# First chunk handed over from SBUF to SBUF at every step of the first batch's head, and weight sums on VectorE

## The chip, the cores and the metric

One NeuronCore of a Trainium2 chip runs the whole kernel. The metric is the device time of the program in microseconds; a time of "the kernel" is the median of several executions. The profile is of one further execution.

## What is computed

Two blocks stand one behind the other: a filter in the frequency domain over each sequence (8 batches of 3008 tokens, 256 channels), and a gated feed-forward block over all 24064 tokens (width 256 to 1536 and back). All is float32; the three weights arrive as float64.

```python
def _attn_ref(x, filt_r, filt_i):            # x: (8, 3008, 256)
    X = np.fft.rfft(x, axis=1)
    F = (filt_r + 1j * filt_i)[None, :, :]
    y = np.fft.irfft(X * F, n=x.shape[1], axis=1)
    return y.astype(np.float32)

def _moe_ref(x, w_gate, w_val, w_out):       # x: (24064, 256)
    g = x @ w_gate
    silu = g * (1.0 / (1.0 + np.exp(-g)))
    val = x @ w_val
    return (silu * val @ w_out).astype(np.float32)
```

## The kernel before

**The spectral part.** A sequence of 3008 = 47 x 64 tokens is transformed in stages of small matrix products. Stage 1 does the transforms of length 47. Stage 2 does those of length 64 for 24 frequencies `s`, two at a time: twelve middle steps `u` (`N_TWO`). `stage2a` (line 873) multiplies by the table `tb[..., 0]`, and VectorE applies the filter (`f0` holds it); `stage2b` (line 909) multiplies by `tb[..., 1]` and so goes back. Its result, 128 rows of two frequencies, is copied by ScalarE from PSUM to a buffer `g` (four of them, used in turn) and stored to a DRAM tensor `d2`. Stage 3 (`stage3`, line 935) goes back over the length 47, in four chunks of tokens, two halves each; it reads `d2` with another grouping of rows (`load_t4`, line 662), 96 rows of 4 token positions to a half. A chunk yields `y`, the transposed tokens that the feed-forward block works on.

**The head of the first batch.** Nothing of the feed-forward block can start before chunk 0 of batch 0 is through stage 3. The loop at line 1227 runs the twelve steps with `stage2b` four steps behind `stage2a`. For steps 0 to 7 the store to `d2` is issued on the queue of SyncE (SP), for 8 to 11 on ScalarE's. The rows of chunk 0 get into `f0` (which the filter no longer needs there) in three ways: after the loop's last `stage2a` two loads from `d2` are issued for rows 0 to 63 (steps 0 to 7), behind the loop two for rows 64 to 87 (steps 8 to 10), and the last step writes its eight rows straight from `g` to `f0`, in eight transfers of 8 KB, in turn on ScalarE's and SP's queue (line 923). So a row of steps 0 to 10 goes to DRAM and comes back. In a row of `g` lie chunks, halves and token positions in the order of the table.

**What else stands in the head.** `idle` (line 585) issues matrix products that compute nothing. Four of them on a tile of zeros stand behind the loop, and two more on the weight sums `A13` and `A01`, which therefore wait for these sums.

**Preparation of the weights.** The float64 weights are loaded in halves (`load_weights`, line 377) and rounded to float32 in a chain of small operations on VectorE, ScalarE and GpSimd (`round_half`, line 388). For the hidden weights, sums of blocks are kept as well: `combine_weights` (line 460) makes for each of six pairs a sum A, on VectorE, partly with a product on ScalarE, and then B and E. B is computed on GpSimd; E on VectorE for four pairs of the first weight group and on GpSimd otherwise. `Preparation` (line 487) writes this out in ticks: each operation has a tick, each weight follows the last by 4 ticks, and the first of the `w_out` weights by 12. `finish(step)` runs all ticks that are due by a step; `tick` runs one. Ahead of stage 3, `finish(0)` and four more ticks are run. In the main loop (line 1380) the order of all engines is written out in `SCHEDULE`; 20 ticks are spread over it for each step, in step 0 only behind the place `A01`.

**The main loop.** A step is one chunk with one of three groups of hidden columns. `P`, `Q`, `A`, `B`, `E` are products of `y` or of sums of `y` (`combine_sequence`, line 989) with weights; `W` are the products with `w_out`. Each engine takes its instructions in program order, and so do the queues of SP and ScalarE on which transfers are issued.

Of the kernel before, what the change touches and what calls it, by code (L numbers as in the profile page):

```python
# [41 lines left out]
FP32 = mybir.dt.float32  # L42
# [6 lines left out]
B, S, C = 8, 3008, 256  # L49
# [5 lines left out]
NS, NQ = 24, 64  # L55
# [69 lines left out]
def dft_tables():  # L125
# [26 lines left out]
    d[0, :, :, 1] = (-sn * sg).transpose(0, 2, 1)  # L152
    d[1, :, :, 1] = (c * sg).transpose(0, 2, 1)
    d = d.reshape(128, NS, 128)
    de = np.stack([d, d.transpose(2, 1, 0)], 2)

    hi = 2 * np.pi * (np.outer(2 * n1 + 1, s) % (2 * N1)) / (2 * N1)
    scale = np.where(s == 0, 1.0, 2.0) / S
# [45 lines left out]
def kernel(  # L204
# [120 lines left out]
    def add(eng, dst, a, b):  # L325
        return eng.tensor_tensor(out=dst, in0=a, in1=b, op=ALU.add)  # L326

    def sub(eng, dst, a, b):
        return eng.tensor_tensor(out=dst, in0=a, in1=b, op=ALU.subtract)  # L329
# [130 lines left out]
    def combine_weights(g, i, j):  # L460

        d = j - i
        wt_f = weights_of(0, 0, g).rearrange("p s z f -> p s (z f)")
        m = wt_f[:, SLOT[f"A{i}{j}"]]
        ui, uj, yi, yj = [wt_f[:, SLOT[f"{p}{q}"]] for p in "PQ" for q in (i, j)]
        if d == 1:
            pin(negated_sum(m, ui, uj))
        else:
            pin(add(nc.vector, m, ui, uj))
        yield  # L470
        if d > 1:
            pin(nc.scalar.mul(m, m, -1.0 / d))
        yield
        pin(sub(nc.gpsimd, wt_f[:, SLOT[f"B{i}{j}"]], yi, m))
        early = g == 0 and PAIRS_USED.index((i, j)) < 4
        pin(add(nc.vector if early else nc.gpsimd, wt_f[:, SLOT[f"E{i}{j}"]], yj, m))

    def keep_weights(g, piece):

# [7 lines left out]
    class Preparation:  # L487
# [3 lines left out]
        def __init__(self):  # L491
# [9 lines left out]
            for i, (_, (use, *at)) in enumerate(weights):  # L501
                hid, g = use == "hid", at[0] if use == "hid" else at[0] // JB
                by = ((0, 3, 6) if hid else (1, 4, 7))[g]
                b = base[-1] + (4 if i != 2 * len(BLOCKS) else 12) if i else 0
                if i >= N_EARLY:
                    same = [n for n in range(N_EARLY, i) if spot_of(n) == spot_of(i)]
                    k = 2 if spot_of(i) is None else 1
                    last = base[same[-k]] + 8 if same[k - 1:] else 0
                    b = max(b, last + 8)
                    put(max(last, b - 10), lambda i=i: load_weights(i), by)  # L510
                base.append(b)
                if hid and g == NG - 1:
# [78 lines left out]
    class Spectral:  # L591


        def __init__(self, b):
# [3 lines left out]

            self.d2_tokens = self.d2.rearrange("a n c -> (a n) c").rearrange(
                "(n a) c -> n a c", n=N2)  # L600
            self.d2_rows = self.d2.rearrange("a (h n) c -> (a h) n c", h=2)
            self.x, self.t2, self.f, self.tb, self.p, self.t4, self.y = {}, {}, {}, {}, {}, {}, {}
            self.real = {}

# [54 lines left out]
            for u in range(i * n // NV, (i + 1) * n // NV):  # L659
                self.tb[u], self.f[u] = tb0[:, ts(u, NV)], f0[:, ts(u, NV)]  # L660

        def load_t4(self, k, i, part=None):
            if part is not None:

                t = f0[0:NK, ts(i, NH), :]
                r = (slice(0, 64), slice(64, NK - 4 * NV))[part]
                self.load(out=t[r], in_=self.d2_rows[r, ts(i, NH), :])
            else:
                t = t4pool.tile([128, NH, C], FP32, name=f"t4_{self.b}_{k}_{i}", tag="t4")
                at = 2 * k + i  # L670
                if self.b == 0:
                    self.load(out=t[0:NK], in_=self.d2_rows[:, ts(at, NH), :])
                else:

                    rows = self.d2_tokens.rearrange("(h n) a c -> h (n a) c", h=2)
                    rows = rows[:, ts(at, 2 * NS * NH)]
                    for j in range(2):
                        self.load(out=t[64 * j:64 * j + 64, 1],
                                  in_=rows[j, 128 * (1 - j):128 * (1 - j) + 64])
                        self.load(out=t[:, 2 * j], in_=rows[j, 64 * j:64 * j + 128])  # L680
            self.t4[k, i] = t

        def bank(self, name):
# [225 lines left out]
        def stage2b(self, u):  # L909
# [5 lines left out]
                                     rhs=pt[:, i, :], start=True, stop=True))  # L915
            g = self.place("g", u)
            yield
            if self.b == 0 and u == N_TWO - 1:
                for i in range(NV):
                    pin(nc.scalar.copy(out=g[:, i], in_=ps[:, i]))  # L920
                for j in range(4 * NV):
                    i, at = j // 4, 64 * (j // 2 % 2) + 32 * (j % 2)
                    pin((nc.scalar, nc.sync)[j % 2].dma_start(
                        out=f0[4 * NV * u + j:4 * NV * u + j + 1, 0:2 * NH],
                        in_=g[at:at + 2 * NH, i:i + 1]))
            else:
                pin(nc.scalar.copy(out=g, in_=ps))
            queue = nc.scalar if self.b or u >= 8 else nc.sync
            if self.b == 0:
                pin(queue.dma_start(out=self.twos(self.d2, u), in_=g))  # L930
                return
            rows = self.d2_tokens.rearrange("n (p s) c -> (n p) (s c)", p=2)
            pin(queue.dma_start(out=rows[:, ts(u, NV * C)], in_=g.rearrange("q s c -> q (s c)")))

        def stage3(self, k, step):

# [240 lines left out]
    with tc.tile_pool(name="start", bufs=1) as spool0:  # L1177
# [49 lines left out]
        for u in range(N_TWO + lag):  # L1227
# [116 lines left out]
    for b in range(B):  # L1344
# [35 lines left out]
        for step in range(NCHUNK * NG + (b == B - 1)):  # L1380
# [98 lines left out]
```

## Time and profile before

| | |
|---|---|
| median of three runs | 2825.01 us (2822.03 to 2826.37) |
| the profiled execution | 2828.65 us, span of its instructions 2826.7 us |
| PE busy (TensorE matmul) | 2786.0 us, 99% |
| DVE (VectorE) | 1993.1 us, 71% |
| ACT (ScalarE), POOL (GpSimd) | 1564.5 us, 55%; 1578.1 us, 56% |
| head of batch 0: last product of the middle steps starts | 60.05 us |
| first product of stage 3 (`wpd`) | 70.21 us |
| first product of the feed-forward block (`wk`) | 76.82 us |

Times inside the profile count from its first instruction. In a timeline a line has the start, the duration, the engine, the line of the code, the operation, the tile written and the tiles read, and the count of instructions merged; the idle time before it and what ended it stand in brackets. SPq and ACTq are the queues on which SP and ScalarE issue transfers; such a line's duration is the time of issue, not that of the transfer. Names of tiles are the program's, so that `f<-d` is a load of `d2` into `f0`, `d<-x` a store of `g` (which lies in the tile `x0`) to `d2`, `f<-x` the transfer from `g` to `f0`, and `t<-d` a load for a later chunk.

### The profile page before, as it was taken

How to read it: one execution, taken by the hardware profiler on the slowest of the kernel's cores; microseconds unless marked ns; L12 is line 12 of the kernel's file. 1: busy time of each engine (PE TensorE's matmuls, PEld its weight loads, DVE VectorE, ACT ScalarE, POOL GpSimd, SP SyncE). 2: the span in 40 equal slices, each digit the busy share in tenths (PEclk: the TensorE clock that was granted, in tenths of full speed). 3: DMA queues.
4: the chain of work that ended last, by engine and by line, in shares of the span. 5: the costliest groups of instructions: out<-in, count | busy, mean ns of one | idle time of the engine just before them, and what ended most of it. 6: DMA issues, size and time to landing. Idle time of an engine off the chain costs nothing.

```text
span 2826.7 us, 48513 instructions
## 1 busy us (share of the span) xinstructions
PE 2786.0 (99%) x15444; PEld 2318.8 (82%) x15444; DVE 1993.1 (71%) x4567; ACT 1564.5 (55%) x4182; POOL 1578.1 (56%) x1683
## 2 busy tenths in 40 slices
PE   8999999999999999999999999999999999999998
PEld 6877878788888888888888888888888888888887
DVE  7898766767667766677766677667676767666666
ACT  5775445555555555555555555555555555555554
POOL 4886575465545654456644566444665455545544
PEclk9999999999999999999999999999999999999999
DMA  9687866877666776667666676667766777654543
GB/s 238 210 275 248 274 215 213 281 221 235 192 184 203 246 221 180 198 212 237 218 185 197 214 242 205 186 192 233 230 207 178 217 222 226 194 149 151 152 137 82
DMA packets 363477, 586.59 MB, mean 208 GB/s; under 512 B 198444, under 2 KB 246380, under 8 KB 363128
## 3 DMA queue, kind: packets, MB, share of 16 engines
q1 hardware_dynamic: 337962, 534.70, 60.9%
q10 hardware_dynamic: 23470, 45.46, 5.9%
q0 software_dynamic: 1792, 3.34, 0.4%
q8 instruction: 125, 2.05, 0.3%
q14 instruction: 128, 1.05, 0.1%
HBM read 467.81 MB, written 101.34 MB: 201 GB/s over the span
## 4 chain that ended last, share of the span: by engine, by line
PE 88%; POOL 3%; DVE 1%; issue 1%; DMA 1%; ACT 0%; ACTq 0%; SPq 0%; POOLq 0%; DVEq 0%
PE wa L1050 24%; PE wk L1050 16%; PE wA L1147 16%; PE we L1050 12%; PE wG L1147 8%; PE wF L1147 4%; PE pd L953 3%; PE wqa L700 2%; PE wqc L759 1%; PE wqb L771 1%; POOL out_dram L1132 1%; POOL h L329 1%; POOL y_t L326 0%; DMA lent<-later_tbl 0%; POOL h L326 0%
## 5 line engine op out<-in xcount | busy, mean ns | idle before, releaser
L1050 PE MATMUL wa<-y_t,wt_t 128*128 128x188 f32 x4464 | 879.5, 323 | 6.1 <-DMA y_t<-yt 1.9
L1050 PEld LDWEIGHTS wa<-y_t,wt_t 128*128 128x128 f32 x4464 | 747.2, 190 | 83.1 <-ACT wa L1076 10.8
L1050 PEld LDWEIGHTS wk<-y,wt_t 128*128 128x128 f32 x2976 | 496.6, 191 | 110.8 <-issue 33.4
L1050 PE MATMUL wk<-y,wt_t 128*128 128x188 f32 x2976 | 573.5, 326 | 5.0 <-DVE y L326 2.8
L326 POOL TENSOR_TENSOR h<-h 128x376 f32<-128x376 f32 x190 | 183.3, 986 | 694.5 <-DVE h L1097 694.5
L329 POOL TENSOR_TENSOR h<-h 128x376 f32<-128x376 f32 x572 | 558.8, 998 | 15.4 <-DVE h L326 15.2
L1147 PE MATMUL wA<-h,wo_t 128*128 128x376 f32 x1532 | 552.3, 483 | 3.6 <-DVE o L326 3.5
L1050 PE MATMUL we<-y_t,wt_t 128*128 128x188 f32 x2232 | 431.8, 323 | 0.7 <-ACT we L1081 0.7
L329 POOL TENSOR_TENSOR D<-f,f 128x376 f32<-128x376 f32 x288 | 279.8, 986 | 258.6 <-ACT f L1065 258.5
L329 DVE TENSOR_TENSOR we<-we,m 128x376 f32<-128x376 f32 x576 | 319.4, 555 | 136.5 <-PE we L1050 70.1
L1050 PEld LDWEIGHTS we<-y_t,wt_t 128*128 128x128 f32 x2232 | 369.5, 190 | 1.5 <-ACT we L1081 1.2
L1147 PEld LDWEIGHTS wA<-h,wo_t 128*128 128x128 f32 x1532 | 275.5, 190 | 113.3 <-issue 6.2
L1085 ACT COPY m<-wa 128x376 f32<-128x376 f32 x576 | 272.6, 473 | 103.0 <-PE wa L1050 100.2
L333 DVE SCALAR_TENSOR_TENSOR y<-wk,c 128x376 f32<-128x376 f32 x480 | 244.4, 539 | 61.4 <-ACT c L1069 39.0
L1092 ACT ACTIVATE g<-wa 128x188 f32<-128x188 f32 x576 | 187.6, 326 | 165.8 <-PE wa L1050 155.3
L1092 ACT ACTIVATE u<-we 128x188 f32<-128x188 f32 x576 | 188.2, 327 | 160.1 <-DVE we L329 153.3
L1147 PE MATMUL wG<-h,wo_t 128*128 128x376 f32 x768 | 274.0, 479 | 0.0
L1069 ACT COPY c<-wk 128x376 f32<-128x376 f32 x288 | 136.4, 473 | 224.8 <-PE wk L1050 189.2
L1065 ACT ACTIVATE f<-wk 128x376 f32<-128x376 f32 x288 | 140.4, 488 | 171.1 <-PE wk L1050 124.3
L1081 ACT COPY we<-y 128x376 f32<-128x376 f32 x480 | 222.2, 480 | 19.6 <-DVE h L1097 13.9
L1097 DVE TENSOR_TENSOR h<-wa,g 128x188 f32<-128x188 f32 x576 | 198.5, 345 | 37.1 <-ACT g L1092 36.8
L1097 DVE TENSOR_TENSOR h<-we,u 128x188 f32<-128x188 f32 x576 | 197.5, 344 | 26.6 <-ACT u L1092 15.6
(165 smaller groups left out, 3515.5 us busy)
## 6 DMA issues: line engine op xcount, KB each, us to landing
wt_t<-w_all SPq DMA_DIRECT2D x174, 896.0 KB
wt_t<-w_all SPq DMA_DIRECT2D x174, 768.0 KB
lent<-filter SPq DMA_DIRECT2D x36, 1024.0 KB
lent<-d SPq DMA_DIRECT2D x84, 256.0 KB
d<-lent ACTq DMA_DIRECT2D x84, 256.0 KB
d<-lent ACTq DMA_DIRECT2D x96, 192.0 KB
lent<-raw SPq DMA_DIRECT2D x144, 128.0 KB
t<-d SPq DMA_DIRECT2D x112, 128.0 KB
```

Of the source, the lines that this page charges most:

```text
L326: return eng.tensor_tensor(out=dst, in0=a, in1=b, op=ALU.add)
L329: return eng.tensor_tensor(out=dst, in0=a, in1=b, op=ALU.subtract)
L333: return nc.vector.scalar_tensor_tensor(out=dst, in0=a, scalar=-1.0, in1=b, op0=ALU.mult, op1=ALU.subtract)
L953: pin(nc.tensor.matmul(out=rows, lhsT=self.t4[k, i][:, j, ts(cb, 128)], rhs=cols, start=j == 0, stop=True, skip_group_check=True))
L1050: pin(nc.tensor.matmul(out=ps[:, z], lhsT=self.wt[:, SLOT[p], z], rhs=rhs, start=start and z == 0, stop=True, skip_group_check=True))
L1065: pin(act.mul(self.small(f"f{i}", f"f{i}", 1), t[f"k{i}"], -1.0))
L1069: pin(act.copy(out=self.small(f"c{i}", f"c{i}", 1), in_=t[f"k{i}"]))
L1081: pin(act.copy(out=self.bank(f"e{at}"), in_=t[f"y{at}"]))
L1085: pin(act.copy(out=self.small(f"m{at}", "m", 4), in_=t[f"a{at}"]))
L1092: pin(act.activation(out=self.small(op, "g", 3, 1)[:, 0], in_=ps[:, 1], func=AF.Silu))
L1097: pin(v.tensor_tensor(out=dst, in0=ps[:, 0], in1=g, op=ALU.mult))
L1147: pin(nc.tensor.matmul(out=self.tiles[at], lhsT=wo_t[:, JB * q + i, WO[p], :], rhs=self.hs[i][:, HID[p]], start=start and i == 0, stop=Tru ...
```

## The change

The columns of the going-back table are put into another order, so that the 32 rows of one chunk lie together in `g`. Every middle step of batch 0 now writes its rows of chunk 0 from `g` to `f0` itself, in two transfers of 32 partitions to 4 rows (32 KB each). They are issued on SP, only the second one of the last step on ScalarE. The stores to `d2` remain, all on SP, for the other chunks: for steps 0 to 8 right behind the two transfers, for 9 to 11 together behind the loop. The loads of chunk 0 from `d2` and the eight transfers of the last step are gone. In `d2` a row of a chunk has eight token positions side by side, and `load_t4` reads it so.

B and E of the first weight group are computed on VectorE for all six pairs. The four early `w_out` halves are loaded at step 10 of the loop instead of step 6. Four ticks are no longer run ahead of stage 3: the `w_out` weights begin 16 instead of 12 ticks behind the hidden ones, and in step 0 ticks begin behind the place `P0` instead of `A01`. The two idle products on `A13` and `A01` are gone.

```diff
     d = d.reshape(128, NS, 128)
-    de = np.stack([d, d.transpose(2, 1, 0)], 2)
+    chunks = np.arange(128).reshape(2, 2, NCHUNK, NW).transpose(2, 0, 1, 3).ravel()
+    de = np.stack([d, d.transpose(2, 1, 0)[:, :, chunks]], 2)
...
-        pin(sub(nc.gpsimd, wt_f[:, SLOT[f"B{i}{j}"]], yi, m))
-        early = g == 0 and PAIRS_USED.index((i, j)) < 4
-        pin(add(nc.vector if early else nc.gpsimd, wt_f[:, SLOT[f"E{i}{j}"]], yj, m))
+        e = nc.gpsimd if g else nc.vector
+        pin(sub(e, wt_f[:, SLOT[f"B{i}{j}"]], yi, m))
+        pin(add(e, wt_f[:, SLOT[f"E{i}{j}"]], yj, m))
...
-                b = base[-1] + (4 if i != 2 * len(BLOCKS) else 12) if i else 0
+                b = base[-1] + (4 if i != 2 * len(BLOCKS) else 16) if i else 0
...
-            self.d2_rows = self.d2.rearrange("a (h n) c -> (a h) n c", h=2)
+            flat = self.d2.rearrange("a n c -> (a n) c")
+            self.d2_parts = flat.rearrange("(s q) c -> q s c", q=128)
+            self.d2_rows = flat.rearrange("(s k a n) c -> k s a n c", k=NCHUNK, a=4, n=NW)
+            self.rest = []
...
-        def load_t4(self, k, i, part=None):
-            if part is not None:
-
-                t = f0[0:NK, ts(i, NH), :]
-                r = (slice(0, 64), slice(64, NK - 4 * NV))[part]
-                self.load(out=t[r], in_=self.d2_rows[r, ts(i, NH), :])
+        def load_t4(self, k, i):
+            t = t4pool.tile([128, NH, C], FP32, name=f"t4_{self.b}_{k}_{i}", tag="t4")
+            at = 2 * k + i
+            if self.b == 0:
+                self.load(out=t[0:NK].rearrange("p (o n) c -> p o (n c)", o=1),
+                          in_=self.d2_rows[k, :, :, ts(i, NH)].rearrange("s a n c -> s a (n c)"))
...
-            if self.b == 0 and u == N_TWO - 1:
+            if self.b == 0:
+                last = u == N_TWO - 1
+                for i in range(0, NV, 1 if last else NV):
+                    n = slice(i, i + (1 if last else NV))
+                    pin(nc.scalar.copy(out=g[:, n], in_=ps[:, n]))
                 for i in range(NV):
-                    pin(nc.scalar.copy(out=g[:, i], in_=ps[:, i]))
-                for j in range(4 * NV):
-                    i, at = j // 4, 64 * (j // 2 % 2) + 32 * (j % 2)
-                    pin((nc.scalar, nc.sync)[j % 2].dma_start(
-                        out=f0[4 * NV * u + j:4 * NV * u + j + 1, 0:2 * NH],
-                        in_=g[at:at + 2 * NH, i:i + 1]))
-            else:
-                pin(nc.scalar.copy(out=g, in_=ps))
-            queue = nc.scalar if self.b or u >= 8 else nc.sync
-            if self.b == 0:
-                pin(queue.dma_start(out=self.twos(self.d2, u), in_=g))
+                    r = 4 * (NV * u + i)
+                    queue = nc.scalar if last and i else nc.sync
+                    pin(queue.dma_start(out=f0[r:r + 4, 0:2 * NH], in_=g[0:4 * NW, i:i + 1]))
+                self.rest.append((u, g))
+                if u < 9:
+                    self.store_rest()
                 return
...
+        def store_rest(self):
+
+            for u, g in self.rest:
+                self.load(out=self.d2_parts[:, ts(u, NV)], in_=g)
+            self.rest = []
...
             if u == 6:
                 pin(nc.sync.dma_start(out=wi_t, in_=wi_dram.ap()))
+            if u == 10:
                 for i in range(8, N_EARLY):
                     load_weights(i)
-            if u == N_TWO - 1:
-                for i in range(2):
-                    spec.load_t4(0, i, 0)
         for i in range(2):
-            spec.load_t4(0, i, 1)
+            spec.t4[0, i] = f0[0:NK, ts(i, NH), :]
+        spec.store_rest()
         for i in range(2):
             spec.load_t4(1, i)
         preparation.finish(0)
-        preparation.tick(0, 4)
 
         idle(zero, [bank("idle") for _ in range(4)], 512)
-        for p in ("A13", "A01"):
-            at = SLOT[p]
-            idle(wt_t[:, at:at + 2].rearrange("p s z f -> p (s z f)"), [bank("idle")], 512)
...
-                        (step or place > SCHEDULE.index("A01")):
+                        (step or place > SCHEDULE.index("P0")):
                     preparation.tick(step)
```

More of the change, by code (lines that the diff above doesn't have):

```diff
@@ L660, in load_tables @@
                 self.tb[u], self.f[u] = tb0[:, ts(u, NV)], f0[:, ts(u, NV)]
-        def load_t4(self, k, i, part=None):
-            if part is not None:
-                t = f0[0:NK, ts(i, NH), :]
-                r = (slice(0, 64), slice(64, NK - 4 * NV))[part]
-                self.load(out=t[r], in_=self.d2_rows[r, ts(i, NH), :])
-            else:
-                t = t4pool.tile([128, NH, C], FP32, name=f"t4_{self.b}_{k}_{i}", tag="t4")
-                at = 2 * k + i
-                if self.b == 0:
-                    self.load(out=t[0:NK], in_=self.d2_rows[:, ts(at, NH), :])
-                else:
[L675 to L680, printed above, removed]
+        def load_t4(self, k, i):
[4 more added lines that the diff above has]
+                          in_=self.d2_rows[k, :, :, ts(i, NH)].rearrange("s a n c -> s a (n c)"))
+            else:
+                rows = self.d2_tokens.rearrange("(h n) a c -> h (n a) c", h=2)
+                rows = rows[:, ts(at, 2 * NS * NH)]
+                for j in range(2):
+                    self.load(out=t[64 * j:64 * j + 64, 1],
+                              in_=rows[j, 128 * (1 - j):128 * (1 - j) + 64])
+                    self.load(out=t[:, 2 * j], in_=rows[j, 64 * j:64 * j + 128])
             self.t4[k, i] = t
@@ L917, in stage2b @@
             yield
-            if self.b == 0 and u == N_TWO - 1:
-                for i in range(NV):
-                    pin(nc.scalar.copy(out=g[:, i], in_=ps[:, i]))
-                for j in range(4 * NV):
-                    i, at = j // 4, 64 * (j // 2 % 2) + 32 * (j % 2)
-                    pin((nc.scalar, nc.sync)[j % 2].dma_start(
-                        out=f0[4 * NV * u + j:4 * NV * u + j + 1, 0:2 * NH],
-                        in_=g[at:at + 2 * NH, i:i + 1]))
-            else:
-                pin(nc.scalar.copy(out=g, in_=ps))
-            queue = nc.scalar if self.b or u >= 8 else nc.sync
-            if self.b == 0:
-                pin(queue.dma_start(out=self.twos(self.d2, u), in_=g))
+            if self.b == 0:
[3 more added lines that the diff above has]
+                    pin(nc.scalar.copy(out=g[:, n], in_=ps[:, n]))
+                for i in range(NV):
+                    r = 4 * (NV * u + i)
[4 more added lines that the diff above has]
+                    self.store_rest()
                 return
+            pin(nc.scalar.copy(out=g, in_=ps))
+            queue = nc.scalar
             rows = self.d2_tokens.rearrange("n (p s) c -> (n p) (s c)", p=2)
             pin(queue.dma_start(out=rows[:, ts(u, NV * C)], in_=g.rearrange("q s c -> q (s c)")))
+        def store_rest(self):
+            for u, g in self.rest:
+                self.load(out=self.d2_parts[:, ts(u, NV)], in_=g)
+            self.rest = []
         def stage3(self, k, step):
```

## The prediction

> **What bounds the kernel now.** First the busy table of the page: TensorE (PE) is busy 2786.0 of 2826.7 us, so only a stretch in which it waits can give anything back. Next the busy times by stretch, for the head of the first batch. Columns: the stretch, its length, then busy us (and instructions) of PE, its weight loads, VectorE (DVE), ScalarE (ACT), GpSimd (POOL), PE's granted clock, DMA share, GB/s.
>
> ```profile
> 62.00:64.60 2.60, 2.60 (x7) 0.83 (x5) 0.00 (x0) 0.30 (x2) 0.00 (x0) 1.00 0.81 217
> 64.60:67.40 2.80, 0.01 (x1) 0.00 (x0) 0.01 (x1) 0.46 (x2) 0.00 (x0) 1.00 0.36 100
> 67.40:70.20 2.80, 2.17 (x4) 0.62 (x5) 2.80 (x4) 1.89 (x5) 2.77 (x4) 1.00 0.75 198
> 70.20:74.00 3.80, 3.78 (x32) 3.63 (x32) 3.80 (x6) 0.83 (x2) 3.80 (x5) 1.00 0.98 254
> 74.00:76.80 2.80, 0.00 (x0) 0.00 (x0) 1.72 (x6) 2.17 (x6) 0.33 (x1) 0.85 0.61 142
> 76.80:80.00 3.20, 3.18 (x13) 3.18 (x14) 1.80 (x4) 1.62 (x4) 1.78 (x2) 0.50 0.00 0
> ```
>
> From 61.0 to 76.8 PE does real work only in 70.2 to 74.0 (the stage-3 products `wpd`); the other 5.8 us that it shows are idle products on zeros and weights. Then the timeline of PE and of ACT says who holds it.
>
> ```profile
> 61.02 3.60 PE L588 MATMUL widle<-room 128*128 128x512 f32 x8
> 67.41 2.17 PE L588 MATMUL widle<-wt_t 128*128 128x512 f32 x4 [2.79 <-ACT wt_t L472]
> 70.21 3.78 PE L956 MATMUL wpd<-wi_t,f 96*128 96x94 f32 x32 [0.63 <-PE widle L588]
> 76.82 1.62 PE L1050 MATMUL wk<-y,wt_t 128*128 128x188 f32 x4 [2.83 <-DVE y L326]
> ```
>
> ```profile
> 61.65 0.65 ACT L920 COPY x<-wpc 128x256 f32<-128x256 f32 x2 [0.51 <-PE wpc L914]
> 62.05 4.17 ACTq L923 DMA_DIRECT2D f<-x  x4
> 66.51 0.38 ACTq L930 DMA_DIRECT2D d<-x  x1
> 66.94 0.42 ACT L472 ACTIVATE wt_t<-wt_t 128x256 f32<-128x256 f32 x1 [4.64 <-DMA f<-x]
> ...
> 74.52 0.51 ACT L419 ACTIVATE pw<-pw,off_t 128x256 f32<-128x256 uint32 x1 [1.12 <-DVE pw L406]
> 75.06 0.51 ACT L421 ACTIVATE pw<-pw,top_t 128x256 f32<-128x256 f32 x1
> 75.60 0.42 ACT L423 ACTIVATE pw<-pw 128x256 uint32<-128x256 f32 x1
> 75.92 0.83 ACT L968 COPY y<-wpd 128x376 f32<-128x376 f32 x2
> ```
>
> Two holds are seen. **The data**: the last `f<-d` loads are issued at 67.40 and 67.87 (SP's timeline), the second for 0.34 us, and `wpd` starts at 70.21, 2.0 us after that issue ended. **The queue of ACT**: its four hand-over transfers and the store keep it 4.64 us from the weight sum L472, on which DVE (5.98 us idle), POOL (8.55) and the second group of idle products wait; and after `wpd` it runs three weight-rounding operations (74.52 to 76.02) before the copy L968 that opens the way to `wk`. The price of a transfer's issue comes from the list of one tile's instructions (ns min/median/max):
>
> ```profile
> L606 SPq DMA_DIRECT2D f<-in_filt_i_dram x6: 311/317/382, 36.8 to 46.1; - x6
> L923 SPq DMA_DIRECT2D f<-x x4: 634/652/772, 62.2 to 66.7; - x4
> ```
>
> And that of a sum on DVE with and without POOL at work beside it (POOL starts at 67.43):
>
> ```profile
> 67.39 0.42 DVE L326 TENSOR_TENSOR wt_t<-wt_t 128x256 f32<-128x256 f32 x1 [5.98 <-ACT wt_t L472]
> 67.73 0.95 DVE L333 SCALAR_TENSOR_TENSOR wt_t<-wt_t 128x256 f32<-128x256 f32 x1
> ```
>
> **What the Trainium skill says.** (1) "TensorE: Matmul & The Clock Gate", "What's actually happening": the clock is halved after an idle window of about 3.4 us, the windows run freely, and a busy one restores it. The trace agrees: the clock is 0.80 over 70 to 80 and 0.86 over 80 to 90, which is 6.8 us at half, two windows. (2) "SBUF — State Buffer", "Who interferes with whom": a DVE instruction with two SBUF inputs contends with GpSimd reads. The trace agrees: 0.42 against 0.95 us. (3) "DMA: Bandwidth & Descriptors", "Why a DMA increments its semaphore by 16 and not by 1": the number of DMA engines is the largest up to 16 that divides the outer dimension of both sides. For a transfer of 32 partitions into 4 that would be 4 engines. No view of before names an engine, so this is open; it carries a rival.
>
> **The change part by part.**
>
> *Hand-overs.* Each of 12 steps now issues two transfers of 32 KB (32 partitions into 4 rows of `f0`), 23 on SP and 1 on ACT; the eight of 8 KB in the last step and the four `f<-d` loads go. What is queued ahead of the last one on SP, from 46.8 us, where SP is done with the table loads: 22 hand-overs, 9 stores (0.37 us and 0.09 to the next, 4.1 us), `wi` and four weight loads (2.2 us). A hand-over's issue isn't shown. Below: 0.32 us, as the 32-row table load; above: 0.65, as the 8-row one. I take 0.36, near the 32-row load and the store, because both have as many rows or more. With 0.09 between: 22 x 0.45 = 9.9, so SP is through at 46.8 + 6.3 + 9.9 = 63.0. (At 0.32: 62.1. At 0.65: 69.4.) The last copy has a second condition: its buffer is that of step 7, whose store sits behind the four weight loads moved from step 6 to step 10. In the window 59 to 62 us, 544 packets of 1 KB took 51.0% of 16 engines' 3 us, 45 ns each, so 256 KB takes 0.72 us: the weights, issued from about 57.4, hold the engines some 2.9 us, and the store of step 7 lands near 63. Copy of one half 0.4, issue 0.36, landing 2.0: **`wpd` starts at 66.0 instead of 70.2**. Within the steps nothing else is bound by it: DVE paces them (0.72 us each for three operations, no idle from 46 to 60).
>
> *Ticks and sums.* The four ticks behind the head go to step 0, after P0 instead of A01 (15 ticks where there were 11). With them the three ACT operations of 74.5 to 76.0 leave the way, and only one rounding operation of DVE stays. B and E sums run on DVE: from the first ACT sum (about 64.5) twelve operations of 0.34 (0.42 less the overlap), 4.1 us, until 68.7; POOL is silent, so none takes 0.95. `wpd` needs 3.6 us and the DVE addition with it 0.4: `wk` at 66.0 + 4.0 = 70.0, where it was 76.8: **-6.8 us**. The cover of the sums is `wpd` itself; were it gone, they would cost up to 1 us. The four sums of the last two pairs cost DVE some 1.4 to 3.8 us in step 0, beside PE's weight-bound first products.
>
> *Clock.* PE's gap shrinks to 64.6 to 66.0, too short for an idle window, although the two idle products on weights are gone. The 28 products of 76.8 to 82.8 ran at 0.31 instead of 0.16 us (0.21 instead of 0.11), 2.9 us. But POOL's four sums (78.2 to 83.2) and its D behind them hold A01 anyway: I take **-1.0** (0 to -2.9).
>
> *Given back.* The first weight of `w_out` starts 4 ticks later, and what is due at step 1 is done there in one piece: seven ticks instead of three. PE waits there already ("PE wF L1147 <- POOL wo_t L438: 1.7, 1, 1.7"), behind POOL's product (0.8 us) and DVE's L426 and L430. I take **+1.0** (0 to +2.5).
>
> *Stores and loads.* The stores of steps 9 to 11 and the loads of chunk 1 follow on SP; loaded at about 70 to 71 instead of 73 to 75, they are covered.
>
> Sum: -6.8 - 1.0 + 1.0 = -6.8. The profiled execution took 2828.65 us (span 2826.7), 3.6 above the median of 2825.0 of three runs; 2821.9 in its terms, **2818** in those of the median.
>
> **Next late** are DVE and POOL: from 86 to 176 they are busy about 84 and 82 of 90 us, PE about 85.
>
> **The rivals.**
> *R1, few engines.* If four engines carry every hand-over, each has 8 packets of 45 ns, 0.36 us: 24 of them 8.6, nine stores 6.5, weights 2.6, sum 17.7 us behind the table loads that fill the engines until about 50.3. The last lands at 69.5. PE is then idle from 64.6 with no product to keep the clock, and `wpd` runs at half for most of its length (5.7 us): `wk` at 75.6, -1.2; clock later -1.0, burst +1.0: 2824. For it: the skill's rule, and a DMA share of 0.9 to 1.0 up to 56 us. Against: the table traffic ends at 51 and the share in 58 to 62 is 0.61.
> *R2, the issue decides: slower.* If a hand-over costs SP 0.65 to 0.8 us, like the 8-row ones, SP is through at 69.4 to 72.8. `wpd` starts at 72.1 to 75.6, at half clock: `wk` at 78.2 to 81.7, +1.4 to +4.9; the burst +1.0; chunk 1, whose loads wait for three stores issued later still, +0 to +1: about 2830. It is slower than before from 0.59 us per issue on. For it: the only SBUF-to-SBUF row of the head. Against: the 32-row rows.
> *R3, lost later.* `wk` comes early, but the full DVE and POOL of 96 to 176 give half of it back: 2821.5.
>
> **Chances.** Forecast 0.55 (2814 to 2820.5), R3 0.07, R1 0.24, R2 0.14. About 0.2% (5.6 us, 2819.4) is what a measurement of this kernel can tell from no change. Of the forecast 0.48 lies beyond it and 0.07 within; R3, R1 and 0.03 of R2 within; 0.11 of R2 beyond. Faster 0.48, same 0.41, slower 0.11. The range runs from 2814 to 2828: it takes in forecast, R3 and R1 and leaves out most of R2.
>
> **What would show it.** Right: issues of `f<-x` on SP near 0.36 us, `wpd` near 66, no half clock before 90, DVE sums of 0.42 ending before `wk` near 70, PE's wait for `wo_t` at step 1 under 3 us. Wrong: SP's issues without a pause up to 69 (R2); packets still moving between issue and a late landing (R1); a PE gap over 3.4 us before `wpd`; new PE waits for DVE or POOL between 90 and 180 (R3).

## The result, and the profile after

The changed kernel takes **2838.83 us** (median of five, 2835.47 to 2839.97) where the kernel before, on the same chip, took 2826.37 (five, 2822.03 to 2828.53): 12.5 us more, ratio 1.0041 with a 95% interval of 1.003 to 1.0053. Forecast was 2818; the range ended at 2828. Its profiled execution took 2839.97 us, with a span of 2838.0.

First PE's timeline of the changed kernel, from the end of the middle steps on (start, duration, line, tiles, count, idle time before it and what ended it):

```profile
61.06 4.25 PE L589 MATMUL widle<-room 128*128 128x512 f32 x8
75.26 7.11 PE L962 MATMUL wpd<-wi_t,f 96*128 96x94 f32 x32 [9.96 <-DMA f<-x]
82.16 1.52 PE L1056 MATMUL wk<-y,wt_t 128*128 128x188 f32 x4
```

`wpd` starts at 75.26 us (70.21 before) and takes 7.11 instead of 3.78; `wk` starts at 82.16 (76.82 before). PE waits 9.96 us for `f<-x`, the hand-overs. Next SP's timeline, and behind it the instructions of the hand-over's line (ns min/median/max):

```profile
59.49 1.32 SPq L925 DMA_DIRECT2D f<-x  x2
60.86 0.44 SPq L610 DMA_DIRECT2D d<-x  x1
61.42 1.34 SPq L925 DMA_DIRECT2D f<-x  x2
62.80 0.44 SPq L610 DMA_DIRECT2D d<-x  x1
63.35 1.84 SPq L387 DMA_DIRECT2D wo_t<-in_moe_w_out_dram  x4
65.28 1.32 SPq L925 DMA_DIRECT2D f<-x  x2
66.65 0.46 SPq L610 DMA_DIRECT2D d<-x  x1
67.22 1.30 SPq L925 DMA_DIRECT2D f<-x  x2
68.57 0.45 SPq L610 DMA_DIRECT2D d<-x  x1
69.12 3.43 SPq L925 DMA_DIRECT2D f<-x  x5
```

```profile
L925 SPq DMA_DIRECT2D f<-x x23: 625/631/830, 47.4 to 71.9; - x23
L925 ACTq DMA_DIRECT2D f<-x x1: 1425/1425/1425, 71.2 to 71.2; - x1
```

A pair of hand-overs takes 1.30 to 1.34 us, a store 0.45, and from 59.5 to 72.55 us no gap is over 0.12 us: SP does nothing but issue. The Trainium skill, "Perfetto Trace Analysis", "DMA Instruction — HWDGE (DVE, Sync)", says that such a line runs from when all semaphores are satisfied to when the sequencer is free again, descriptors generated, and that the movement of data is not in it. The trace agrees: the last hand-over on SP is issued from 71.93 to 72.55 us and its semaphore rises for the last time at 74.92. So 0.63 us is the price on SP itself, not that of the transfer.

The busy times by stretch, here by tens (columns as in the prediction), carry the clock. Before:

```profile
70.00:80.00 10.00, 6.96 (x45) 6.83 (x46) 7.52 (x14) 4.62 (x11) 6.11 (x8) 0.80 0.56 139
80.00:90.00 10.00, 9.98 (x58) 9.62 (x58) 5.97 (x13) 6.55 (x19) 8.02 (x10) 0.86 0.70 248
100.00:110.00 10.00, 8.32 (x43) 6.49 (x42) 10.00 (x21) 7.59 (x21) 9.84 (x12) 1.00 0.66 225
```

Changed kernel:

```profile
60.00:70.00 10.00, 5.11 (x13) 2.03 (x12) 0.98 (x3) 1.76 (x3) 0.00 (x0) 0.94 0.70 230
70.00:80.00 10.00, 4.74 (x22) 4.77 (x23) 3.98 (x12) 2.32 (x6) 0.00 (x0) 0.50 0.37 118
80.00:90.00 10.00, 10.00 (x41) 9.63 (x40) 3.94 (x9) 3.16 (x8) 5.89 (x5) 0.53 0.74 213
110.00:120.00 10.00, 5.17 (x17) 4.07 (x16) 7.70 (x13) 4.90 (x13) 9.42 (x13) 0.66 0.66 237
```

Between 70 and 90 us the clock is 0.50 and 0.53, where it was 0.80 and 0.86. By the trace's clock records it was half from 68.8 to 89.3 us, 20.5 us instead of 6.8, and once more from 113.2 to 120.0 us, where it was full before.

This is not all. Set against the kernel before by the n-th product, PE is about 6.5 us late up to the first product with `w_out` at step 1, 11.9 us late a few us behind it and 11.3 us at the end. PE's timeline there, first the kernel before and then the changed one:

```profile
103.21 0.80 PE L1147 MATMUL wF<-h,wo_t 128*128 128x376 f32 x2
105.69 0.90 PE L1147 MATMUL wF<-h,wo_t 128*128 128x376 f32 x2 [1.68 <-POOL wo_t L438]
```

```profile
109.72 0.80 PE L1153 MATMUL wF<-h,wo_t 128*128 128x376 f32 x2
115.35 1.62 PE L1153 MATMUL wF<-h,wo_t 128*128 128x376 f32 x2 [4.83 <-DMA y<-y]
```

The waits of the changed kernel (us in total, times, longest):

```profile
PEld wF L1153 <- POOL wo_t L439: 5.4, 1, 5.4
PE wF L1153 <- DMA y<-y: 4.8, 1, 4.8
```

In the kernel before they were 2.3 and 1.7. The second line names a DMA; the first, of the same product, names what came last: POOL's product for the rounded weight. POOL's timeline, before:

```profile
99.70 0.77 POOL L438 TENSOR_TENSOR wo_t<-w,pw 128x256 f32<-128x256 f32 x1
100.43 1.37 POOL L326 TENSOR_TENSOR y_t<-y 128x564 f32<-128x564 f32 x1
101.88 1.45 POOL L329 TENSOR_TENSOR y_t<-y_t,y 128x564 f32<-128x564 f32 x1
103.29 1.55 POOL L326 TENSOR_TENSOR y_t<-y_t,y 128x564 f32<-128x564 f32 x1
104.81 0.82 POOL L438 TENSOR_TENSOR wo_t<-wo_t,pw 128x256 f32<-128x256 f32 x1
```

And in the changed kernel:

```profile
108.93 1.38 POOL L327 TENSOR_TENSOR y_t<-y 128x564 f32<-128x564 f32 x1
110.39 1.39 POOL L330 TENSOR_TENSOR y_t<-y_t,y 128x564 f32<-128x564 f32 x1
111.74 1.42 POOL L327 TENSOR_TENSOR y_t<-y_t,y 128x564 f32<-128x564 f32 x1
113.12 0.91 POOL L439 TENSOR_TENSOR wo_t<-w,pw 128x256 f32<-128x256 f32 x1
114.45 0.84 POOL L439 TENSOR_TENSOR wo_t<-wo_t,pw 128x256 f32<-128x256 f32 x1 [0.42 <-DVE wo_t L431]
```

A weight of `w_out` takes two such products, one for each half. Before, the first of the second weight stood ahead of the three sums (99.70 us) and only the second behind them (104.81); now both stand behind, and the second waits for DVE besides. PE went on at 105.69 us before and goes on at 115.35 now, 2.5 and 5.6 us behind the first product with `w_out`. The longer wait is the larger part of this loss. The rest is the clock, at half behind it: from there to the second `wk` (109.86 and 121.78 us) PE takes 6.4 us instead of 4.2.

So there are two losses, one in the head and one at step 1, and each has a wait and a stretch at half clock.

### The profile page after: what moved, and what is told of

Its sections match the earlier page's. It is cut to its first block, busy times and chain, and to the rows that moved or that the text cites. A ratio compares the mean times of both kernels' runs of the same rounds, so it can differ in the third digit from the quotient of the medians.

```text
span 2838.0 us, 48517 instructions
## 1 busy us (share of the span) xinstructions
PE 2790.8 (98%) x15440; PEld 2324.0 (82%) x15440; DVE 1993.3 (70%) x4575; ACT 1565.7 (55%) x4182; POOL 1571.5 (55%) x1675
## 3 DMA queue, kind: packets, MB, share of 16 engines
q14 instruction: 128, 1.05, 0.1%
## 4 chain that ended last, share of the span: by engine, by line
PE 90%; POOL 4%; DMA 3%; DVE 2%; issue 1%; ACT 1%; SPq 0%; ACTq 0%; POOLq 0%; DVEq 0%
PE wa L1056 24%; PE wk L1056 17%; PE wA L1153 16%; PE we L1056 12%; PE wG L1153 8%; PE wF L1153 4%; PE pd L959 3%; PE wqa L699 1%; PE wqc L758 1%; PE wqb L770 1%; POOL out_dram L1138 1%; POOL h L330 1%; DMA f<-in_filt_r_dram 1%; POOL y_t L327 1%; POOL h L327 0%
## 5 line engine op out<-in xcount | busy, mean ns | idle before, releaser
L330 POOL TENSOR_TENSOR h<-h 128x376 f32<-128x376 f32 x572 | 557.6, 997 | 15.4 <-DVE h L327 15.2
L334 DVE SCALAR_TENSOR_TENSOR y<-wk,c 128x376 f32<-128x376 f32 x480 | 244.4, 539 | 58.1 <-ACT c L1075 36.1
```

What stands on the lines that cost most here:

```text
L334: return nc.vector.scalar_tensor_tensor(out=dst, in0=a, scalar=-1.0, in1=b, op0=ALU.mult, op1=ALU.subtract)
```

## The experiments

Each time is a median, with the ratio to the kernel before on the same chip (2826.0 to 2826.7 us) and its 95% interval. The theory: SP's issues delay the head by some 6 us (rival R2 of the prediction), and the moved ticks cost another 5 to 6 at step 1. Rivals: the bytes of the hand-overs on few DMA engines (R1), the landing of the stores, the sums on VectorE, the clock.

### The ticks

**ticks_back** (the changed kernel, three edits undone):

```diff
-  b = base[-1] + (4 if i != 2 * len(BLOCKS) else 16) if i else 0
+  b = base[-1] + (4 if i != 2 * len(BLOCKS) else 12) if i else 0
+        preparation.tick(0, 4)
-  (step or place > SCHEDULE.index("P0")):
+  (step or place > SCHEDULE.index("A01")):
```

> The changed kernel with its weight ticks put back: w_out begins 12 ticks behind, four ticks run ahead of stage 3, and ticks in step 0 begin behind A01. Hand-overs and sums stay. Theory (two separate losses: SP's hand-over issues of 0.63 us in the head, and the postponed ticks at step 1): PE's wait for wo_t at the start of step 1 goes from 4.8 us back to about 2, the first wpd stays near 75.3, the time falls by 3 to 5 us, to about 2834. Rival (the wait at step 1 is only the late head's echo): the wait stays over 4 us and the time within 1 us of the changed kernel's.

2832.79 us, 1.0017 (1.0009 to 1.0025): 6.0 less than the change. PE's wait at step 1 is 1.7 us again, and the head is as late as in the change (`wk` 82.57).

**ticks_12** undoes only the first line of that diff.

> The changed kernel, but w_out begins 12 ticks behind the hidden weights again; the other two edits of the ticks stay (from P0, none ahead of stage 3). If the late begin of w_out is what makes PE wait at step 1, this alone gives back 4 to 6 us (2833 to 2835). If it is that fewer ticks are run ahead of stage 3, so that they pile up in step 0 all the same, under 1 us comes back.

2834.41 us, 1.0029 (1.0018 to 1.0041), 4.4 less, though this interval overlaps that of the change. In its trace PE's wait at step 1 is 1.8 us again and the clock is full there; so, of the three edits, the late begin of `w_out` is the one that makes the wait.

**before_ticks_late** puts the reverse of the three edits into the kernel before.

> The kernel before with only the four ticks moved (w_out begins 16 ticks behind the hidden weights, ticks of step 0 from P0 on, no four ticks ahead of stage 3). If the ticks cost by themselves, PE's wait for wo_t at step 1 grows from 1.7 to about 5 us and the kernel takes 4 to 6 us more (2830 to 2832); the three ACT operations leave the way to wk, which may come up to 1 us sooner. If they cost only together with the late head, the time is within 1.5 us of before.

2832.38 us, 1.0021 (1.0013 to 1.0029): **6.3 us more, from the ticks alone**, in a kernel whose head is nearly as it was (`wk` 77.09; `wpd` runs at half clock here, 7.11 us, but the gap of 2.83 us behind it is gone). Expected were 4 to 6. Its waits:

```profile
PEld wF L1147 <- POOL wo_t L438: 5.5, 1, 5.5
PE wF L1147 <- DMA y<-y: 4.9, 1, 4.9
```

The clock is at half from 108.4 to 115.2 us here too.

### The sums and the clock

**sums_back** (B and E of the first group on the engines of before):

```diff
-  e = nc.gpsimd if g else nc.vector
-  pin(sub(e, wt_f[:, SLOT[f"B{i}{j}"]], yi, m))
-  pin(add(e, wt_f[:, SLOT[f"E{i}{j}"]], yj, m))
+  pin(sub(nc.gpsimd, wt_f[:, SLOT[f"B{i}{j}"]], yi, m))
+  early = g == 0 and PAIRS_USED.index((i, j)) < 4
+  pin(add(nc.vector if early else nc.gpsimd, wt_f[:, SLOT[f"E{i}{j}"]], yj, m))
```

> The changed kernel with B and part of E of the weight sums back on GpSimd as before; nothing else. Theory: the sums lie in a stretch where VectorE waits 12 us for nothing else, so they cost nothing on either engine: within 1 us of the changed kernel. Rival (the four sums that VectorE now does in step 0 feed the late work at step 1): the time falls by 1 to 3 us.

2836.82 us, 1.0039 (1.0026 to 1.0051); its interval and that of the change overlap, and the 2.0 us less would fit the rival's 1 to 3 as well. By the trace little of it is in the head (`wk` 0.2 us sooner), and behind step 1 PE is 12.3 us late against 11.9. Two kernels below (hybrid11_ticks, one_hand_ticks_early) have the sums on VectorE and take no longer than before. So the sums are not where the 12 us went; whether they cost a us or two isn't decided.

**warm** (16 idle products ahead of `wpd` instead of four):

```diff
-  idle(zero, [bank("idle") for _ in range(4)], 512)
+  idle(zero, [bank("idle") for _ in range(16)], 512)
```

> The changed kernel with 16 instead of 4 idle products on zeros ahead of stage 3, so that PE has something to do until about 75; nothing else. Theory (half clock is a consequence worth several us): the clock stays full until wpd, its 32 products take 3.6 instead of 7.1 us, wk starts 3 to 4 us earlier and the time falls by 3 to 5 us. Rival (the short products of wpd do not hold the clock up, whatever runs ahead): wpd is fast, but the clock falls again behind it, and the gain is under 3 us.

2836.32 us, 1.0035 (1.0022 to 1.0047). PE's timeline shows where the gain went:

```profile
75.75 3.78 PE L962 MATMUL wpd<-wi_t,f 96*128 96x94 f32 x32
79.36 0.83 PE L1056 MATMUL wk<-y,wt_t 128*128 128x188 f32 x4
85.64 2.02 PE L962 MATMUL pd<-wi_t,t 96*128 96x94 f32 x8 [5.45 <-DMA t<-d]
```

`wpd` takes 3.78 us and `wk` comes 2.8 us sooner, but PE then waits 5.45 us for chunk 1's rows, whose loads stand behind the last stores, and the clock falls again (84.3 to 91.1 us): PE, 2.5 us late at `wk`, is 8.45 us late some ten us on, where the change is 6.5 late. So the head gained nothing, and the interval overlaps that of the change. Behind the hand-overs, chunk 1's loads are next late.

### What holds the hand-overs

**two_queues** (the second hand-over of every step on ACT's queue):

```diff
-  queue = nc.scalar if last and i else nc.sync
+  queue = nc.scalar if i else nc.sync
```

> The changed kernel with the second hand-over of every step on ScalarE's queue instead of SP's; nothing else. Theory (SP's issues in a row set the landing): SP sheds 11 issues of 0.68 us, the last hand-over is issued near 65 and wpd starts at 67 to 69 instead of 75.3; the half-clock stretch shortens; the time falls by 6 to 9 us, to about 2831. Rival (the four DMA engines that carry a hand-over are the bound): the landing stays within 2 us of 75, and so does the time within 2 us of the changed kernel's.

2840.45 us, 1.0048 (1.0036 to 1.0061). A miss: `wpd` at 78.25 is later still, not sooner. Of the rival's two numbers the time came true (1.6 us from the change) and the landing did not. ACT's copies wait for stores in order, 4.94 us at step 4 and 5.19 at the last, and hand-overs behind them on the same queue wait too. So fewer issues on SP do not help where they block ACT.

**weights_early** (the four `w_out` loads at step 6 again):

```diff
-            if u == 10:
```

> The changed kernel, but the four w_out loads stand at step 6 again, so the store of step 7, for whose buffer the last step's copy waits 4.40 us, is no longer behind them. If SP's row of issues is the bound (22 x 0.68 + 9 x 0.5 + 5 x 0.45 us from 46.3 on), SP is through near 68 instead of 72.5, the first wpd product starts near 71 to 72 instead of 75.3, and the kernel takes 3 to 4 us less (about 2835). If it is the landing of the transfers, the weights only hold the engines earlier: wpd stays at 75 and the time at 2838 to 2839.

2837.04 us, 1.0035 (1.0023 to 1.0046). ACT's last copy, in the changed kernel and here:

```profile
70.57 0.65 ACT L921 COPY x<-wpc 128x256 f32<-128x256 f32 x2 [4.40 <-DMA d<-x]
```

```profile
70.05 0.65 ACT L921 COPY x<-wpc 128x256 f32<-128x256 f32 x2 [1.32 <-DMA d<-x]
```

It no longer waits 4.40 us for the store of step 7, but 1.32; yet `wpd` starts at 75.06. SP issues without a pause to 72.43, as in the change. So that store, which my prediction held for a second condition, did not set the end. My expectation of SP through near 68 and `wpd` at 71 to 72 failed: SP's work is the same, only in another order.

**stores_act** (stores of steps 0 to 8 on ACT's queue):

```diff
-  self.load(out=self.d2_parts[:, ts(u, NV)], in_=g)
+  pin((nc.scalar if u < 9 else nc.sync).dma_start(
+      out=self.d2_parts[:, ts(u, NV)], in_=g))
```

> The changed kernel, but the stores of steps 0 to 8 are issued on ScalarE's queue, so SP issues 22 hand-overs and five loads alone and no store stands behind the weight loads. If SP's row of issues is the bound: 9 x 0.5 = 4.5 us less, wpd near 71, about 2834. If instead the landing of earlier transfers holds every issuing queue, ScalarE blocks in front of a store as it did with the second hand-over there (4.9 us behind d<-x), and wpd stays at 75 or later, 2838 to 2841.

2841.23 us, 1.005 (1.0037 to 1.0063), `wpd` at 78.44: as the rival said, landings. The trace gives each transfer one of eight completion semaphores in turn; SP's hand-over of 60.07 carries that of an ACT store that landed at 60.05, the one of 61.86 that of a store that landed at 61.84. So here an issue waits for the transfer that last used its semaphore, whichever queue it was on.

**half_hand** (for steps 0 to 10 only the first hand-over):

```diff
-  for i in range(NV):
+  for i in range(NV if last else 1):
```

> The changed kernel, but of steps 0 to 10 only the first of the two hand-overs is issued (half of chunk 0's rows of these steps is left out; all other work stays). If the number of hand-over issues sets the head, SP has 11 x 0.68 = 7.5 us less to issue: wpd near 68 and the end near 69, wk 6 to 8 us earlier than 82.2, and about 2831. If the tail from the last copy through issue to landing sets it, wpd moves by under 2 us and the time stays above 2836.

2831.58 us, 1.0019 (1.0013 to 1.0026), 7.3 less than the change: `wpd` 69.27, `wk` 76.17. With eleven transfers fewer (11 x 0.68 = 7.5) the head is where it was before. But this halves the bytes as well, and leaves out half of the rows of chunk 0; alone it does not tell the issues from the bytes.

**micro_issue** measures the price by itself. Columns: ns min/median/max, first and last start; the view's other lines are left out.

> Leaves out the whole computation and only issues transfers, six of each form (the last two forms of load four), behind each other. If the number of rows of a hand-over or its 1 KB pieces made its issue dear, 32 rows to 32 rows costs 0.6 us too and 4 rows of 8 KB to 4 rows 0.3. If it is the different grouping of rows on the two sides, only the forms 32 to 4, 8 to 1, 128 to 16 and the load of 24 by 4 rows cost 0.6 us or more, and 32 to 32, 4 to 4, plain loads and stores 0.3 to 0.45. If it is SBUF on both sides, 32 to 32 and 4 to 4 cost 0.6 and no load or store does. On ACT's queue 32 to 4 costs 1.2 to 1.4 if its 1.27 us in the head are its own price, 0.6 if it waited there.

```profile
L47 SPq DMA_DIRECT2D to_sp_r32to__63<-from_sp_r32to__61 x6: 611/628/837, 5.2 to 8.7; - x6
L47 ACTq DMA_DIRECT2D to_act_r32to__169<-from_act_r32to__166 x6: 636/637/1214, 41.3 to 45.8; - x6
L51 SPq DMA_DIRECT2D to_sp_r8to__85<-from_sp_r8to__82 x6: 620/634/687, 15.7 to 30.4; - x6
L55 SPq DMA_DIRECT2D to_sp_r32to__74<-from_sp_r32to__71 x6: 587/588/589, 11.8 to 15.0; - x6
L59 SPq DMA_DIRECT2D to_sp_r4to__96<-from_sp_r4to__93 x6: 584/592/647, 31.1 to 46.4; - x6
L63 SPq DMA_DIRECT2D to_sp_r128to__107<-from_sp_r128to__104 x6: 598/602/633, 48.6 to 51.9; - x6
L68 SPq DMA_DIRECT2D to_sp_load__118<-in_x_dram x6: 311/419/732, 52.5 to 55.3; - x6
L73 SPq DMA_DIRECT2D to_sp_load__129<-in_x_dram x6: 248/293/299, 56.4 to 58.6; - x6
L84 SPq DMA_DIRECT2D to_sp_load__140<-in_x_dram x4: 318/408/424, 59.0 to 60.3; - x4
L90 SPq DMA_DIRECT2D to_sp_load24by__149<-in_x_dram x4: 773/804/891, 60.7 to 63.4; - x4
```

From above: SBUF to SBUF 32 rows to 4 (SP, then ACT), 8 to 1, 32 to 32, 4 to 4, 128 to 16; loads from DRAM of 32 rows, 4 rows, 96 rows, and 96 rows regrouped as 24 by 4. **Every SBUF-to-SBUF form costs 0.59 to 0.63 us, from 8 KB to 128 KB and with or without regrouping; a plain load 0.29 to 0.42.** Of the load, regrouping doubles the price (0.80 against 0.41), which is that of `t<-d` in the changed kernel (0.82; 0.39 each before).

**one_hand** keeps all bytes and halves the issues: ACT copies the 32 rows of both frequencies under each other into a small tile (three buffers), one transfer of 64 KB takes them over.

```diff
-  pin(queue.dma_start(out=f0[r:r + 4, 0:2 * NH], in_=g[0:4 * NW, i:i + 1]))
+  h = hand[:, u % 3]
+  for i in range(NV):
+      pin(nc.scalar.copy(out=h[ts(i, 4 * NW)], in_=ps[0:4 * NW, i]))
+  r = 4 * NV * u
+  pin(nc.sync.dma_start(out=f0[r:r + 4 * NV, 0:2 * NH], in_=h))
+  pin(nc.scalar.copy(out=g, in_=ps))
```

> The changed kernel, but a step's two hand-overs are one transfer of 64 KB (64 partitions to 8 rows), out of a small tile into which ACT first copies the 32 rows of both frequencies (two more copies per step); every byte still goes, SP issues 12 instead of 23. If SP's issues are the bound (0.63 us each), SP has 11 x 0.68 less, wpd starts near 68 to 69 instead of 75.3, as where half the rows were left out, and the kernel takes 6 to 8 us less (2831 to 2833). If the bytes on few DMA engines are the bound, wpd stays at 73 or later and the time at 2836 or more.

2835.28 us, 1.0026 (1.0017 to 1.0035), `wpd` at 74.40. By the numbers of the expectation this speaks for the bytes. The timelines of ACT and SP name another wait:

```profile
69.33 0.75 ACT L920 COPY hand<-wpc 32x256 f32<-32x256 f32 x2 [4.13 <-DMA f<-hand]
```

```profile
62.09 1.86 SPq L387 DMA_DIRECT2D wo_t<-in_moe_w_out_dram  x4
64.04 0.61 SPq L922 DMA_DIRECT2D f<-hand  x1
```

The copy waits for its buffer, whose transfer was issued at 64.04 behind the four weight loads: with SP free, the weights moved to step 10 hold the tail. The next runs take them away.

### Versions that might beat both

**hybrid11_ticks**: only the last step hands over (two transfers), rows of steps 0 to 10 go through `d2`, stores, weights and ticks are as before (`first_rows` loads the rows of the given steps from `d2` into `f0`).

```diff
-  for i in range(NV):
+  for i in range(NV if u >= 11 else 0):
...
+  spec.first_rows(i, 0, 8)
...
+  spec.first_rows(i, 8, 11)
```

> The permuted columns and the sums on VectorE as changed, but only the last step hands its rows over, in its two transfers; rows of steps 0 to 10 go through d2 as before, stores and weight loads stand on the queues and at the steps of before, and the four ticks are run ahead of stage 3 again. If the number of hand-overs and the moved ticks are all that cost, this keeps what the change was good for: two issues (1.3 us) instead of four plus four on ACT and SP (4.2 us on ACT), wpd near 68, wk near 74, 2822 to 2825 where before takes 2826.5. If the new column order or the d2 layout costs as well (loads of t<-d take 0.8 us to issue), it is slower than before: 2828 to 2832.

2825.75 us, 0.9993 (0.9984 to 1.0001): the time of before. `wpd` starts at 71.50: the loads of the rows of steps 8 to 10 stand on SP behind the last hand-over, are issued at 66.69 and 67.50, and the first lands at 71.25. They do not wait for the store of step 10, which had landed at 65.92, though the next expectation says so.

**hybrid8_sp_ticks**: the same with 8 for 11, no second loads, all eight transfers on SP.

> New column order, sums on VectorE, ticks as before; steps 8 to 11 hand over (all eight transfers on SP, 0.68 us each), rows of steps 0 to 7 are loaded from d2 as before, stores and weight loads at the places of before. The last f<-d load no longer waits for a store of step 10, and ACT issues no hand-over (1.3 us there against 0.63 on SP). If the count of issues behind the last copy sets the start: copy at 65.0, two issues until 66.4, landing 2.5 us later, wpd near 68.5 to 69 and 2821 to 2824. If hand-overs of four steps in a row already pile up on SP (1.4 us of each 1.9 us step and the two loads of 0.8), wpd is at 71 to 72 and the time that of before, 2825 to 2828.

2828.06 us, 1.0005 (0.9997 to 1.0013), `wpd` at 72.12: the second case. The eight hand-overs stand on SP behind two loads of `d2` that wait for a store, and begin at 63.25.

**one_hand_ticks** is one_hand with the ticks of before.

> One transfer per step as in one_hand, and the ticks as in the kernel before. If issues and ticks are the whole loss, both gains add up: wpd near 69 (70.2 before), wk near 74 to 76, PE's wait for wo_t at step 1 at 1.7 us, and 2823 to 2827. If something else in the change costs as well (sums on VectorE, the lost idle products on the weight sums, the order of columns), 2829 to 2832.

2829.96 us, 1.0011 (1.0003 to 1.0019); `wpd` at 72.07, held by the weights as in one_hand.

**one_hand_ticks_early** has the weights at step 6 besides.

> As one_hand_ticks, with the four w_out loads at step 6 again. With SP no longer full, the store of step 7 behind the weight loads would hold the last copies next: then wpd comes 1 to 3 us sooner than in one_hand_ticks and the time is 1 to 3 us less. If not, the two agree within 1.5 us.

2824.45 us, 0.9992 (0.9984 to 1.0): 5.5 less than one_hand_ticks, the fastest of all, but against before the interval reaches 1. PE's timeline:

```profile
70.77 3.78 PE L960 MATMUL wpd<-wi_t,f 96*128 96x94 f32 x32 [0.64 <-ACT pw L424]
75.37 0.90 PE L1054 MATMUL wk<-y,wt_t 128*128 128x188 f32 x4 [0.82 <-DVE y L327]
```

All twelve steps hand over all their bytes, and `wk` starts at 75.37, 1.45 us sooner than before: the bytes are not the bound that they seemed in one_hand. But these transfers, of 64 partitions to 8 rows, go over eight engines where those of the change go over four (so the rises of their semaphores say, see R1 below), so this run does not rule out R1; the change's own trace does, below. Here ACT is the bound, with 1.33 us of copies per step.

### One sum over all runs

With late ticks put at 6.3 us (before_ticks_late) and the rest at the shift of `wk` in the profiled execution, against the medians:

| kernel | `wk` against 76.82 | ticks | sum | measured |
|---|---|---|---|---|
| the change | +5.3 | +6.3 | +11.6 | +12.5 |
| two_queues | +8.3 | +6.3 | +14.6 | +13.8 |
| stores_act | +8.5 | +6.3 | +14.8 | +15.2 |
| weights_early | +5.1 | +6.3 | +11.4 | +11.0 |
| sums_back | +5.1 | +6.3 | +11.4 | +10.2 |
| warm | +2.5 | +6.3 | +8.8 | +9.7 |
| one_hand | +4.5 | +6.3 | +10.8 | +8.6 |
| half_hand | -0.7 | +6.3 | +5.6 | +5.6 |
| ticks_back | +5.8 | 0 | +5.8 | +6.2 |
| one_hand_ticks | +2.2 | 0 | +2.2 | +3.3 |
| hybrid8_sp_ticks | +2.2 | 0 | +2.2 | +2.0 |
| hybrid11_ticks | +1.0 | 0 | +1.0 | -0.3 |
| one_hand_ticks_early | -1.5 | 0 | -1.5 | -2.2 |

The two losses add up to within 1.3 us, but for one_hand (2.2). The row of warm agrees by chance, since the gain at `wk` is lost again ten us later. ticks_12 has no row: what its one edit leaves of the ticks' cost was not measured apart.

## Why the prediction was wrong

- **The price of an issue.** "I take 0.36, near the 32-row load and the store, because both have as many rows or more." This step failed. The chosen neighbour was like in rows; the 8-row transfer (0.65, the upper bound) was like in where data lie, and micro_issue shows that this decides. On its own, 22 x (0.63 - 0.36) = 5.9 us. R2 was the mechanism that came true, its times in part by luck. It had SP ready for the last hand-over at 69.4 to 72.8 (71.93), `wpd` at 72.1 to 75.6 (75.26) and `wk` at 78.2 to 81.7 (82.16, half a us beyond), but for a price of 0.65 to 0.8. With 0.63 the same sum gives 46.8 + 6.3 + 22 x 0.72 = 68.9. The other 3 us are small terms that it lacked: the first hand-over began at 47.41, SP waited twice (1.36 and 0.51 us), and a store took 0.45, not 0.37.
- **"Within the steps nothing else is bound by it: DVE paces them."** From 59.5 us on SP is the one without a gap, at 1.9 us a step; the last copies waited for stores that it had issued.
- **The second condition**, the store of step 7 behind the weights: the wait is there (4.40 us), but weights_early took it away and `wpd` stayed. It decides only where SP has room (one_hand_ticks against one_hand_ticks_early, 5.5 us).
- **Given back: "+1.0 (0 to +2.5)".** The mechanism was the one named, seven ticks in one piece at step 1 behind POOL's product; the size was not. It is 6.3 us in before_ticks_late. Both of POOL's products for the second weight now stand behind three sums of the next chunk (4.2 us), so PE goes on 3.2 us later there (5.7 instead of 2.5 us behind the first product with `w_out`), and half clock behind that wait adds 2.5 (6.6 instead of 4.2 us to the second `wk`). I had not written out POOL's order, and had no clock in this term. With this term, R2 was 2830 + 5.3, about 2835; my range had no case for both.
- **Clock -1.0.** The miss follows from the first step: half clock for 20.5 us instead of none. `wpd` at 7.11 instead of 3.78 us is part of the shift of `wk`. The prediction's reading that the trace of before agrees with a window of 3.4 us holds for the length at half only: there the clock fell at 75.97 us, 1.98 us behind the end of `wpd`, in a gap of 2.83 us in all. So its "too short for an idle window" had less ground than it seemed; no run tested the gap of 1.4 us that it forecast.
- **Sums on VectorE at no cost.** The mechanism was right: they take 0.42 us each with POOL silent, also the operation of L334, of the kind that took 0.95 beside POOL, and end at 77.1, beside `wpd`. The cost of nothing is not shown to better than 2 us (sums_back).
- **R1, four engines.** The number was right, the consequence not. By the Trainium skill, "DMA: Bandwidth & Descriptors", "Why a DMA increments its semaphore by 16 and not by 1", each engine that a transfer uses posts one rise and the issuing sequencer writes the rest at once. The trace agrees with four engines: a hand-over's semaphore rises once some 1.05 us after the issue begins and then four times, a store's sixteen times. But four engines carried what SP issued: from the begin of an issue to the last rise it takes 3.2 us for the hand-over of 59.49, up to 4.3 behind the four weight loads, and 3.3, 3.2, 3.1, 2.9 and 3.0 for the last five on SP. Were the engines the bound, landing would fall ever further behind issue. (R1's sum also puts the weights at 2.6 us, where the forecast has 2.9.)

## What to carry to other kernels

Price a transfer by where its two ends lie before its rows or bytes: here SBUF to SBUF cost 0.59 to 0.63 us to issue whatever it moved, so fewer and larger ones are what helps (one_hand_ticks_early). Before work is deferred "by four ticks", write out the order of the engine on which it lands; what counts is what has got ahead of it, not its own length. And a longer route can cost nothing while it is hidden: with the rows of eleven of the twelve steps going through DRAM (the kernel before, hybrid11_ticks) the time was within 0.1% of that with all handed over directly (one_hand_ticks_early).

## What the runs showed of the hardware

- An SBUF-to-SBUF issue has one price from 8 to 128 KB (0.59 to 0.63 us); a load of 96 rows from DRAM costs 0.80 regrouped and 0.41 plain.
- On ACT's queue the only hand-over of the change took 1.43 us; in micro_issue the first took 1.21 and the others 0.64, in the kernel before (8 KB each) the first 1.26 and the others 0.63 to 0.64. Why the first one is dearer stays open.
- 32 products of 94 columns, back to back for 7.11 us, did not bring a halved clock back (the change, half_hand, before_ticks_late); it came back only with the 188-column products behind them. By the Trainium skill, "TensorE: Matmul & The Clock Gate", "What's actually happening", one busy window of about 3.4 us restores it. These products did not do so here. Yet they held a clock that was full: in one_hand_ticks_early the same 32 ran from 70.77 to 74.55 us at full clock, and it fell only at 77.60. No run settled why the two differ.
